# Moving the row maximum of a random-feature attention from a subtraction on k to a factor on v, with the k projection as row-tiled pairs and two load buffers for v

## The chip, the cores and the metric

The kernel runs on one core of one Trainium2 chip. The metric is the device time of one execution in microseconds (us), told as the median of several runs. The profile is one execution, recorded by the hardware profiler. PE is TensorE (PEld its weight loads), DVE is VectorE, ACT is ScalarE, POOL is GpSimd, SP is SyncE (here only an issuer of DMAs).

## The reference, cut to what matters

Eight batches of eight heads, 576 rows of 64 numbers each, go through random-feature attention (128 features), then through a gated feed-forward layer of 512 to 1536 to 512.

```
def phi(x):                       # x already scaled
    proj = einsum('bhsd,md->bhsm', x, omega)
    h = proj - sum(x * x, -1) / 2
    return exp(h - max(h, -1)) / sqrt(m)
q_p, k_p = phi(q), phi(k)
kv  = einsum('bhsm,bhsd->bhmd', k_p, v);   z = sum(k_p, axis=2)
num = einsum('bhsm,bhmd->bhsd', q_p, kv);  den = einsum('bhsm,bhm->bhs', q_p, z)
x   = num / den                   # then (gelu(x Wg) * (x Wv)) Wo
```

The term `sum(x*x)/2` is the same for all features of a row, so it falls out of `h - max(h)`. For q the whole maximum cancels in `num / den`. For k it does not: each row s carries a factor exp(-max of row s), which has to be either in the features or, as in the change, on the rows of v and on the column of ones that gives z.

## The kernel before: the parts that matter

The ones column is the 65th column of each head of `v_ext`, so one matmul gives both kv and z. PSUM is split: `att` has two buffers for all attention results, `mo` has four for the feed-forward layer.

```
ld   = tile_pool("ld", bufs=2);  work = tile_pool("work", bufs=2)
att  = tile_pool("att", bufs=2, space=PSUM);  mo = tile_pool("mo", bufs=4, space=PSUM)

def load_kq(b):  # k then q of a batch, f32 in HBM to bf16, issued by GpSimd on its queue
    ...
def load_v(b):   # f32, issued by SyncE on its own queue, ONE buffer; cast by GpSimd
    vf  = ld.tile([P, H, R * D], F32, name="vf", bufs=1)
    vrf = ld.tile([P, 4, D], F32, name="vrf", bufs=1)
    nc.sync.dma_start(out=vf, in_=v[b, ...])
    ...
    nc.gpsimd.tensor_copy(ve[:, :, :, :D], vf...)      # v_ext, its ones column set once
    ...

kq = {0: load_kq(0)};  vx = {0: load_v(0)}
...
kq[1] = load_kq(1);  vx[1] = load_v(1)

def k_feat(ps, dst, n):
    nmax = work.tile([P, n, 1], F32, name="nmax", bufs=4)
    nc.vector.reduce_max(nmax, ps, axis=AX, negate=True)
    kd = work.tile([P, n, M], F32, name="kd", bufs=5)
    nc.vector.tensor_add(kd, ps, nmax.broadcast_to((P, n, M)))
    nc.scalar.activation(dst, kd, func=Exp)

for hp in range(H // 2):                               # four groups of k rows
    pk = att_tile([P, 8, M], F32, "pk")
    for i in range(4):                                 # omega2T: omega twice, block diagonal
        nc.tensor.matmul(pk[:, 2*i:2*i+2, :], kT[:, 4*hp+i, :], omega2T)
    k_feat(pk, k_p[...], 8)
pkr = ...                                              # the last 64 rows of each head, the same
if not on_dma:                                         # batches 0 and 1 only
    qT = transpose_main(q_in, "q")                     # TensorE transposes into an att buffer
for hp in range(H // 2):                               # q features: a row-tiled pair each
    for r2 in range(2):
        sl = slice(r2 * D, (r2 + 1) * D)
        nc.tensor.matmul(pq[:, r2, :], omegaT2[sl], qT[sl, 4*hp:4*hp+4, :])
    nc.scalar.activation(q_pT[...], pq, func=Exp)
...                                                    # kz = k_p^T [v, 1], then nd = q_p kz
attention(0)
for t in range(9):                                     # the steady part
    load of batch t+2; attention(t+1); project_out(t-1); gate_val(t)
```

The softmax here doesn't subtract the row's maximum and nothing guards it: scores larger than these inputs give would overflow.

## Time and profile before

| | before |
|---|---|
| median time | 399.5 us (3 runs, 398.19 to 399.78; the prediction starts from it) |
| PE busy | 355.4 us, 89% of the span |
| DVE busy | 224.2 us, 56% |
| k rows on DVE: reduce / subtract | 32 x 1216 ns / 32 x 1215 ns |
| first projection of k (first `pk`) | 17.34 us |
| first `kz` matmul of batch 0 / of batch 1 | 35.48 / 68.09 us |
| one steady pass (from a batch's first `pk` to the next's) | 38.19 us |

The page of the kernel before: the busy line of its part 1; two of the slice lines (each digit is a fortieth of the span, in tenths: PE's busy share and the granted clock of TensorE); the chain of waits; three groups (line, engine, operation, output<-input, shape, count, then busy us and mean ns of one, then the idle time before and who ended it).

```profile
PE 355.4 (89%) x2212; PEld 174.2 (44%) x2249; DVE 224.2 (56%) x345; ACT 154.6 (39%) x202; POOL 63.0 (16%) x87
...
PE   0446756999999999999999999999999999999995
...
PEclk9999985899999999999999999999999999999999
...
PE 80%; DVE 9%; DMA 4%; issue 2%; ACT 2%; POOL 1%; SPq 0%; DVEq 0%; POOLq 0%
...
L219 DVE TENSOR_REDUCE nmax<-pk 128x8 f32<-128x1024 f32 x32 | 37.6, 1216 | 1.1 <-PE pk L227 1.1
L221 DVE TENSOR_TENSOR kd<-pk,nmax 128x1024 f32<-128x1024 f32 x32 | 37.5, 1215 | 0.0
...
L227 PE MATMUL pk<-omega2T,kT 128*128 128x256 bf16 x128 | 20.0, 294 | 5.0 <-DVE kd L221 4.9
```

From the eighth slice on PE is at 9 tenths: there the kernel is mostly bound by matmuls, and an engine such as DVE has time to spare on average. Only the first seven slices, about 70 us, are a chain of dependences, and the timeline shows what it is made of. The lines below are start, length, engine, line, what, count, and in brackets how long the engine had been idle and what ended that.

```profile
17.18 0.37 PE L206 MATMUL rT_ps<-ident,q_in 128*128 128x128 bf16 x2 [3.79 <-DMA q_in<-in_q_dram]
17.34 1.91 PE L227 MATMUL pk<-omega2T,kT 128*128 128x256 bf16 x8
...
18.44 2.36 DVE L219 TENSOR_REDUCE nmax<-pk 128x8 f32<-128x1024 f32 x2 [0.43 <-PE pk L227]
20.71 2.35 DVE L221 TENSOR_TENSOR kd<-pk,nmax 128x1024 f32<-128x1024 f32 x2
...
21.99 2.17 PE L227 MATMUL pk<-omega2T,kT 128*128 128x256 bf16 x8 [2.73 <-DVE kd L221]
...
27.82 1.87 PE L187 MATMUL qT_ps<-ident,q_in 128*128 128x128 bf16 x16 [0.61 <-DVE kd L221]
```

PE waits for the last of q (17.18), fills both attention buffers (17.34), and then stands until DVE has reduced and subtracted (21.99). Everything after follows DVE, up to the transposes of q at 27.82, which need one of the same two buffers.

### The profile page before, as it was taken

Reading aid. Unit: us, or ns where it says so; the run is one execution under the profiler, and the core shown is the slowest. Engines: PE = TensorE matmul, PEld = TensorE weight load, DVE = VectorE, ACT = ScalarE, POOL = GpSimd, SP = SyncE. Lnnn points to the kernel's source line nnn. Section 1 sums busy time; section 2 is a strip of 40 time slices with the busy share of each in tenths; the row PEclk is TensorE's granted clock in tenths of the full one; section 3 lists DMA queues with packets and bytes.
Section 4 is the critical chain, followed back from the end, with each engine's and each line's share of the span. In section 5 each row is a group of like instructions: output and inputs, shape, how many; then the busy total and the mean of one; then the engine's idle time right before and its main releaser. Section 6 shows DMA issues by size and latency. Waiting matters only on the chain.

```text
span 398.3 us, 5658 instructions
## 1 busy us (share of the span) xinstructions
PE 355.4 (89%) x2212; PEld 174.2 (44%) x2249; DVE 224.2 (56%) x345; ACT 154.6 (39%) x202; POOL 63.0 (16%) x87
## 2 busy tenths in 40 slices
PE   0446756999999999999999999999999999999995
PEld 0323523545444544444444444454535444444442
DVE  1392593748574956495559546864776423433332
ACT  1044027234833482447335633653464312311310
POOL 7563422600222041104100200000000000000000
PEclk9999985899999999999999999999999999999999
DMA  9999999980799089909992820371022012002004
GB/s 179 234 213 219 206 232 154 192 157 0 142 158 209 8 144 225 150 11 189 167 150 47 185 49 1 70 176 35 0 88 58 16 33 72 2 27 81 0 10 95
DMA packets 89626, 43.65 MB, mean 110 GB/s; under 512 B 55808, under 2 KB 84992, under 8 KB 89600
## 3 DMA queue, kind: packets, MB, share of 16 engines
q1 hardware_dynamic: 59504, 29.14, 34.2%
q0 software_dynamic: 30096, 14.16, 28.1%
q8 instruction: 17, 0.28, 0.3%
q14 instruction: 9, 0.07, 0.1%
HBM read 37.78 MB, written 9.44 MB: 119 GB/s over the span
## 4 chain that ended last, share of the span: by engine, by line
PE 80%; DVE 9%; DMA 4%; issue 2%; ACT 2%; POOL 1%; SPq 0%; DVEq 0%; POOLq 0%
PE g_ps L327 23%; PE v_ps L333 23%; PE o_ps L357 21%; DVE nmax L219 3%; DMA q_in<-in_q_dram 3%; DVE kd L221 3%; PE pk L227 3%; PE nd L276 2%; PE kz_ps L261 2%; PE pq L243 2%; ACT q_pT L245 2%; DMA out_dram<-o_sb 1%; PE qT_ps L187 1%; DVE x_sb L281 1%; DVE o_sb L360 1%
## 5 line engine op out<-in xcount | busy, mean ns | idle before, releaser
L335 DVE TENSOR_TENSOR gated<-g_gelu,v_ps 128x512 bf16<-128x512 bf16 x108 | 73.8, 683 | 86.2 <-PE v_ps L333 80.9
L330 ACT ACTIVATE g_gelu<-g_ps 128x512 bf16<-128x512 f32 x108 | 64.4, 597 | 141.2 <-PE g_ps L327 133.1
L327 PE MATMUL g_ps<-xT,w_gate_sb 128*128 128x512 bf16 x419 | 116.0, 382 | 1.5 <-issue 0.4
L333 PE MATMUL v_ps<-xT,w_val_sb 128*128 128x512 bf16 x417 | 109.9, 379 | 1.2 <-issue 0.6
L357 PE MATMUL o_ps<-w_out_sb,gated 128*128 128x512 bf16 x423 | 98.6, 379 | 0.4
L222 ACT ACTIVATE k_p<-kd 128x1024 bf16<-128x1024 f32 x32 | 33.8, 1057 | 77.6 <-DVE kd L221 76.4
L333 PEld LDWEIGHTS <-w_val_sb 128*128 128x128 bf16 x432 | 41.3, 98 | 46.9 <-issue 0.5
L357 PEld LDWEIGHTS <-gated 128*128 128x128 bf16 x432 | 41.3, 98 | 45.7 <-issue 2.7
L327 PEld LDWEIGHTS <-w_gate_sb 128*128 128x128 bf16 x432 | 40.3, 98 | 44.6 <-issue 3.7
L360 DVE COPY o_sb<-o_ps 128x512 f32<-128x512 f32 x36 | 24.2, 686 | 40.8 <-PE o_ps L357 21.2
L219 DVE TENSOR_REDUCE nmax<-pk 128x8 f32<-128x1024 f32 x32 | 37.6, 1216 | 1.1 <-PE pk L227 1.1
L221 DVE TENSOR_TENSOR kd<-pk,nmax 128x1024 f32<-128x1024 f32 x32 | 37.5, 1215 | 0.0
L245 ACT ACTIVATE q_pT<-pq 128x1024 bf16<-128x1024 f32 x32 | 30.0, 1023 | 3.9 <-PE pq L243 3.9
L227 PE MATMUL pk<-omega2T,kT 128*128 128x256 bf16 x128 | 20.0, 294 | 5.0 <-DVE kd L221 4.9
L281 DVE TENSOR_TENSOR x_sb<-nd,iden 128x512 bf16<-128x512 f32 x32 | 21.5, 688 | 0.4
L72 POOL DMA_DIRECT2D k_in<-in_k_dram x8 | 7.3, 914 | 80.1 <-DMA kT<-k_in 79.1
L227 PEld LDWEIGHTS <-kT 128*128 128x128 bf16 x128 | 11.8, 103 | 14.4 <-DVE kd L221 11.4
L243 PE MATMUL pq<-qT,omegaT_109 64*128 64x512 bf16 x64 | 13.9, 440 | 4.6 <-DVE qT L190 2.6
L265 DVE CAST kz<-kz_ps 128x520 bf16<-128x520 f32 x8 | 5.6, 698 | 20.0 <-PE kz_ps L261 20.0
L276 PEld LDWEIGHTS <-q_pT 128*128 128x128 bf16 x256 | 11.3, 104 | 9.2 <-DVE x_sb L281 3.8
L276 PE MATMUL nd<-kz,q_pT 128*128 128x65 bf16 x256 | 13.4, 203 | 1.6 <-DVE kz L265 1.2
L72 POOL DMA_DIRECT2D q_in<-in_q_dram x8 | 7.2, 906 | 36.0 <-DMA qT<-q_in 16.4
(69 smaller groups left out, 192.1 us busy)
## 6 DMA issues: line engine op xcount, KB each, us to landing
vf<-in_v_dram SPq DMA_DIRECT2D x8, 1024.0 KB, 8.7
out_dram<-o_sb SPq DMA_DIRECT2D x40, 128.0 KB, 2.4
k_in<-in_k_dram POOLq DMA_DIRECT2D x8, 512.0 KB, 9.1
q_in<-in_q_dram POOLq DMA_DIRECT2D x8, 512.0 KB, 10.6
out_dram<-o_sb SPq DMA_DIRECT2D x16, 256.0 KB, 2.9
w_gate_sb<-in_moe_w_gate_dram POOLq DMA_DIRECT2D x3, 512.0 KB, 15.0
w_val_sb<-in_moe_w_val_dram POOLq DMA_DIRECT2D x3, 512.0 KB, 14.3
w_out_sb<-in_moe_w_out_dram POOLq DMA_DIRECT2D x3, 512.0 KB, 18.9
```

The lines of the kernel that those rows point to most:

```text
L219: nc.vector.reduce_max(nmax, ps, axis=AX, negate=True)
L221: nc.vector.tensor_add(kd, ps, nmax.broadcast_to((P, n, M)))
L222: nc.scalar.activation(dst, kd, func=Exp)
L227: nc.tensor.matmul(pk[:, 2 * i:2 * i + 2, :], kT[:, 4 * hp + i, :], omega2T)
L245: nc.scalar.activation(q_pT[:, hp].rearrange("m a c p -> m a (c p)"), pq, func=Exp)
L276: nc.tensor.matmul(nd[:, h // 4, (h % 4) * DP1:(h % 4 + 1) * DP1], q_pT[:, h // 2, r2, 2 * (h % 2) + rp, :], kz_h(h))
L327: nc.tensor.matmul(g_ps, w_gate_sb[:, jm, fs], xT[:, jm, :], start=(jm == 0), stop=(jm == N_DM - 1))
L330: nc.scalar.activation(g_gelu, g_ps, func=Gelu)
L333: nc.tensor.matmul(v_ps, w_val_sb[:, jm, fs], xT[:, jm, :], start=(jm == 0), stop=(jm == N_DM - 1))
L335: nc.vector.tensor_mul(gated[:, jf, :], g_gelu, v_ps)
L357: nc.tensor.matmul(o_ps, gated[:, jf, qq * P:(qq + 1) * P], w_out_sb[:, jf, :], start=(jf == 0), stop=(jf == N_DFF - 1))
L360: nc.vector.tensor_copy(o_sb, o_ps)
```

## The change

The intent is to take the subtraction (half of what DVE does for k) away. Exp reads the projection straight from PSUM; the maximum is still reduced by DVE, but goes through a small Exp into weights `wk`, with which DVE multiplies v; GpSimd copies them into the ones column (for the last 64 rows DVE does that too). GpSimd's casts of v go. The k projection becomes pairs of 64-row matmuls that can run side by side, as q's was already. Since the cast of v now needs the maximum, v stays in its f32 buffer for longer, and the change gives v two buffers. The diff, cut to its core:

```
     def load_v(b):
-        vf = ld.tile([P, H, R * D], F32, name="vf", bufs=1)
-        vrf = ld.tile([P, 4, D], F32, name="vrf", bufs=1)
+        vf = ld.tile([P, H, R * D], F32, name="vf")          # the pool's two buffers
+        vrf = ld.tile([P, 4, D], F32, name="vrf")
...
-        nc.gpsimd.tensor_copy(ve[:, :, :, :D], vf...)        # and two for vrf
...
-        def k_feat(ps, dst, n): reduce_max, tensor_add, Exp
         for hp in range(H // 2):
-                nc.tensor.matmul(pk[:, 2*i:2*i+2, :], kT[:, 4*hp+i, :], omega2T)
+                for r2 in range(2):
+                    sl = slice(r2 * D, (r2 + 1) * D)
+                    nc.tensor.matmul(pk[:, r2, i, :], kT[sl, 4*hp+i, :], omegaT2[sl])
+            nc.scalar.activation(k_p[:, hp]..., pk..., func=Exp)
+            nc.vector.reduce_max(nmax[:, :, 4*hp:4*hp+4], pk, axis=AX, negate=True)
+            if hp == 2:
+                nc.scalar.activation(wk[:, :, :8], nmax[:, :, :8], func=Exp)
...                                                           # pkr the same
             nc.scalar.activation(q_pT[...], pq, func=Exp)
+            if hp == 0:
+                nc.scalar.activation(wk[:, :, 8:], nmax[:, :, 8:], func=Exp)
...
+        for hh in range(2):
+            isl = slice(8 * hh, 8 * hh + 8)
+            nc.vector.tensor_mul(vei[:, isl, :, :D], vfi[:, isl], wki[:, isl]...broadcast)
+            nc.gpsimd.tensor_copy(vei[:, isl, :, D], wki[:, isl])
...                                                           # v_rbd the same, on DVE
```

More of the change, by code (lines that the diff above doesn't have):

```diff
@@ L89 @@
         nc.vector.memset(v_rbd[i], 0.0)
-        nc.vector.memset(v_ext[i][:, :, :, D:DP1], 1.0)
-        for e in range(2):
-            nc.vector.memset(v_rbd[i][e * SR:(e + 1) * SR, :, e, D:DP1], 1.0)
     def load_v(b):
-        vf = ld.tile([P, H, R * D], F32, name="vf", bufs=1)
-        vrf = ld.tile([P, 4, D], F32, name="vrf", bufs=1)
+        vf = ld.tile([P, H, R * D], F32, name="vf")
+        vrf = ld.tile([P, 4, D], F32, name="vrf")
         nc.sync.dma_start(
@@ L103, in load_v @@
                     .rearrange("j s d -> s j d"))
-        ve, vr = v_ext[b % 2], v_rbd[b % 2]
-        nc.gpsimd.tensor_copy(ve[:, :, :, :D],
-                              vf.rearrange("p h (r d) -> p h r d", r=R))
-        for e in range(2):
-            sl = slice(e * SR, (e + 1) * SR)
-            nc.gpsimd.tensor_copy(vr[sl, :, e, :D], vrf[sl])
-        return ve, vr
+        return vf, vrf
     omega_f = singles.tile([M, D], F32)
@@ L123 @@
     omegaT2 = singles.tile([2 * D, M], BF16)
-    omega2T = singles.tile([2 * D, 2 * M], BF16)
-    nc.vector.memset(omega2T, 0.0)
     for e in range(2):
@@ L128 @@
         nc.vector.tensor_copy(omegaT2[sl], omegaT_ps)
-        nc.vector.tensor_copy(omega2T[sl, e * M:(e + 1) * M], omegaT_ps)
     w_gate_sb = singles.tile([P, N_DM, d_ff], BF16)
@@ L194, in attention @@
         k_both, k_in, k_rest, q_both, q_in, q_rest = kq.pop(b)
-        ve, vr = vx.pop(b)
+        vf, vrf = vx.pop(b)
+        ve, vr = v_ext[b % 2], v_rbd[b % 2]
         on_dma = b > 1
@@ L211, in attention @@
             krT, qrT = rT[:, :2], rT[:, 2:]
-        k_p = work.tile([P, H, R, M], BF16, name="k_p")
-        k_pr = work.tile([P, 4, M], BF16, name="k_pr")
-        def k_feat(ps, dst, n):
-            nmax = work.tile([P, n, 1], F32, name="nmax", bufs=4)
-            nc.vector.reduce_max(nmax, ps, axis=AX, negate=True)
-            kd = work.tile([P, n, M], F32, name="kd", bufs=5)
-            nc.vector.tensor_add(kd, ps, nmax.broadcast_to((P, n, M)))
-            nc.scalar.activation(dst, kd, func=Exp)
+        k_p = work.tile([P, H // 2, 2, 4, M], BF16, name="k_p")
+        k_pr = work.tile([P, 2, 2, M], BF16, name="k_pr")
+        nmax = work.tile([P, 2, 18], F32, name="nmax")
+        wk = work.tile([P, 2, 18], F32, name="wk")
         for hp in range(H // 2):
-            pk = att_tile([P, 8, M], F32, "pk")
+            pk = att_tile([P, 2, 4, M], F32, "pk")
             for i in range(4):
-                nc.tensor.matmul(pk[:, 2 * i:2 * i + 2, :], kT[:, 4 * hp + i, :], omega2T)
-            k_feat(pk, k_p[:, 2 * hp:2 * hp + 2].rearrange("p h r m -> p (h r) m"), 8)
-        pkr = att_tile([P, 4, M], F32, "pkr")
-        for jj in range(2):
-            nc.tensor.matmul(pkr[:, 2 * jj:2 * jj + 2, :], krT[:, jj, :], omega2T)
-        k_feat(pkr, k_pr, 4)
+                for r2 in range(2):
+                    sl = slice(r2 * D, (r2 + 1) * D)
+                    nc.tensor.matmul(pk[:, r2, i, :], kT[sl, 4 * hp + i, :], omegaT2[sl])
+            nc.scalar.activation(k_p[:, hp].rearrange("p a i m -> p a (i m)"),
+                                 pk.rearrange("p a i m -> p a (i m)"), func=Exp)
+            nc.vector.reduce_max(nmax[:, :, 4 * hp:4 * hp + 4], pk, axis=AX, negate=True)
+            if hp == 2:
+                nc.scalar.activation(wk[:, :, :8], nmax[:, :, :8], func=Exp)
+        pkr = att_tile([P, 2, 4, M], F32, "pkr")
+        for jj in range(2):
+            for j2 in range(2):
+                sl = slice(j2 * D, (j2 + 1) * D)
+                nc.tensor.matmul(pkr[:, j2, jj, :], krT[sl, jj, :], omegaT2[sl])
+        nc.scalar.activation(k_pr, pkr[:, :, :2], func=Exp)
+        nc.vector.reduce_max(nmax[:, :, 16:], pkr[:, :, :2], axis=AX, negate=True)
         if not on_dma:
@@ L251, in attention @@
         nc.scalar.activation(q_pTr.rearrange("m a c p -> m a (c p)"), pqr[:, :, :256], func=Exp)
+        vei = ve.rearrange("p h (c r) d -> p (h c) r d", r=2)
+        vfi = vf.rearrange("p h (c r d) -> p (h c) r d", c=2, r=2)
+        wki = wk.rearrange("p r i -> p i r")
+        for hh in range(2):
+            isl = slice(8 * hh, 8 * hh + 8)
+            nc.vector.tensor_mul(vei[:, isl, :, :D], vfi[:, isl],
+                                 wki[:, isl].unsqueeze(3).broadcast_to((P, 8, 2, D)))
+            nc.gpsimd.tensor_copy(vei[:, isl, :, D], wki[:, isl])
+        for e in range(2):
+            sl = slice(e * SR, (e + 1) * SR)
+            vre = vr[sl, :, e, :].rearrange("p (a j) d -> p a j d", j=2)
+            nc.vector.tensor_mul(vre[..., :D],
+                                 vrf[sl].rearrange("p (a j) d -> p a j d", j=2),
+                                 wki[sl, 16:].unsqueeze(3).broadcast_to((SR, 2, 2, D)))
+            nc.vector.tensor_copy(vre[..., D], wki[sl, 16:])
         kz_ps = att_tile([P, 2, 512], F32, "kz_ps")
@@ L256, in attention @@
             g, c0 = j // 2, (j % 2) * 2 * DP1
-            nc.tensor.matmul(kz_ps[:, g, c0:c0 + 2 * DP1], k_pr[:, j, :],
+            nc.tensor.matmul(kz_ps[:, g, c0:c0 + 2 * DP1], k_pr[:, j % 2, j // 2, :],
                              vr[:, j].rearrange("p e c -> p (e c)"), start=True, stop=False)
@@ L261, in attention @@
                     nc.tensor.matmul(kz_ps[:, g, c0 + e * DP1:c0 + (e + 1) * DP1],
-                                     k_p[:, 2 * j + e, r, :], ve[:, 2 * j + e, r, :],
+                                     k_p[:, j, r % 2, 2 * e + r // 2, :], ve[:, 2 * j + e, r, :],
                                      start=False, stop=(e == 1 and r == R - 1))
```

## The prediction

> **What bounds the kernel now.** TensorE (PE): 89% busy on the page, the chain of waits is 67% the three feed-forward lines, and from 74 us on every slice shows 9 tenths. In the timeline one pass (attention of a later batch, project_out, gate_val) takes 38.19 us (o_ps runs begin at 92.74, 130.93, 169.12): 144 feed-forward matmuls at 216 ns are 31.1, attention the other 7.1. Only the head, to 72 us, is a dependency chain: for k of batch 0 VectorE (DVE) runs without gap from 18.44 to 29.0 us (reduce 1216 ns, add 1215 ns, four groups); batch 1 repeats it from 51.14 to 61.7.
>
> **Removed.** The subtraction: 32 x 1215 + 8 x 683 ns = 43 us of DVE; the v casts on GpSimd (21.6 us).
>
> **Added.** Per batch two 1024-element f32 multiplies on DVE (estimate 1.2 us each, as the kd add) and small ones (1 us): DVE falls by some 15 us. Two tiny Exps (estimate 0.25 us each). In the k projection 18 matmuls of 256 columns (108 ns apart in the steady part) become 18 row pairs of 128.
>
> **PE, steady part.** pq is such a pair already: its matmuls begin 3 ns apart, so a k pair should cost 55 to 66 ns (a load plus 65 columns of kz go every 33 ns). Gain 18 x 48 = 0.8 us per batch. But o_ps to pq takes 312 ns in place of 216, and pq to o_ps 320 after a 213 ns stream: 0.2 us per row-tiled run. The Trainium skill, "TensorEngine Tiling (Array Packing)", Key Properties, says that changing mode drains the array; the trace agrees. In the built order the k projection lies in four separate runs per batch: 0.8 us of new switches. Net: I take -0.3 us over six batches.
>
> **Head.** A pk buffer was held for two DVE operations (2.43 us). Now Exp (1.02) and reduce (1.22) read it, and the built order makes the reduce wait for ScalarE. With two buffers, and the first v multiply ahead of the fourth reduce, my schedule frees the last pk buffer 1.7 to 2.0 us earlier per batch, not 5; the extra Exp takes back 0.25. So kz comes 1.5 to 1.8 us earlier after the first pk in batches 0 and 1.
> But v of batch 1 no longer waits for a buffer: its load falls into 10 to 17 us beside k and q of batch 0, and PE starts pk only when the last of q has landed (17.15 us). Estimated slip, by packet rates: 1.2 to 1.7 us. Batch 0 then gains almost nothing.
>
> **Sum.** 399.5 - 0.2 (batch 0) - 1.6 (batch 1) - 0.3 (steady) = about 397.3 us; 8 in 10 between 394.0 and 400.4. Chances: faster by over 2% 0.05, within 0.92, slower 0.03.
>
> **What would show it.** First pk at 18.5 to 19 us, not 17.34. Idle before nmax ended by ScalarE. DVE near 210 us. kz of batch 0 at 35 to 35.6 us (35.48 before), of batch 1 near 66.5 (68.09). A pass of 38.0 to 38.4 us. Switches of 0.1 us at pk.
>
> **What would make it wrong.** Pairs not overlapping (110 ns each: +5 us). q landing unmoved (1.5 us more gain). The half-rate PE clock of 56 to 73 us ending elsewhere (1 to 2 us). A reduce or o_sb copy late in the steady part, stalling PE at pkr or pq, where the schedule leaves about 0.5 us.

## The result, and the profile after

The changed kernel takes 395.34 us (median of 4 runs, 394.74 to 395.64) against 399.25 us (398.19 to 399.78, 4 runs) of the kernel before in the same rounds. The ratio is 0.9903, with a 95% interval of 0.9879 to 0.9928. A ratio here is the mean time of one kernel's fast runs over that of the other's of the same rounds, so not quite the ratio of the medians. The result is correct.

The page of the changed kernel, in the same lines as above:

```profile
PE 353.2 (90%) x2393; PEld 167.8 (43%) x2393; DVE 213.3 (54%) x344; ACT 154.5 (39%) x218; POOL 47.9 (12%) x79
...
PEclk9999975999999999999999999999999999999999
...
PE 86%; DVE 5%; DMA 3%; ACT 3%; issue 1%; POOL 1%; POOLq 0%
...
L214 ACT ACTIVATE k_p<-pk 128x1024 bf16<-128x1024 f32 x32 | 31.9, 1023 | 41.9 <-PE pk L213 41.8
L216 DVE TENSOR_REDUCE nmax<-pk 128x8 f32<-128x1024 f32 x32 | 37.9, 1220 | 13.0 <-ACT k_p L214 13.0
...
L213 PE MATMUL pk<-omegaT_100,kT 64*128 64x128 bf16 x256 | 12.3, 228 | 3.6 <-DVE nmax L216 3.6
```

DVE's share of the chain falls from 9% to 5%, and the wait before the reduce is now for ScalarE (13.0 us) where it was 1.1 us for PE: Exp and reduce read a buffer one after the other. The timeline of the head shows the same, and two things more.

```profile
18.60 0.37 PE L196 MATMUL rT_ps<-ident,q_in 128*128 128x128 bf16 x2 [4.19 <-DMA q_in<-in_q_dram]
18.91 1.19 PE L213 MATMUL pk<-omegaT_100,kT 64*128 64x128 bf16 x16
...
19.56 1.94 ACT L214 ACTIVATE k_p<-pk 128x1024 bf16<-128x1024 f32 x2 [17.53 <-PE pk L213]
20.61 2.35 DVE L216 TENSOR_REDUCE nmax<-pk 128x8 f32<-128x1024 f32 x2 [1.18 <-ACT k_p L214]
21.89 0.61 PE L213 MATMUL pk<-omegaT_100,kT 64*128 64x128 bf16 x8 [1.79 <-DVE nmax L216]
...
24.73 1.22 DVE L254 TENSOR_TENSOR v_ext_70<-vf,wk 128x1024 bf16<-128x1024 f32 x1
...
25.87 1.22 DVE L216 TENSOR_REDUCE nmax<-pk 128x8 f32<-128x1024 f32 x1
...
27.14 1.87 PE L176 MATMUL qT_ps<-ident,q_in 128*128 128x128 bf16 x16 [1.87 <-DVE nmax L216]
```

First, the last of q lands 1.4 us later (18.60 against 17.18). Second, DVE does a multiply of v (24.73) before the last group's reduce (25.87), while PE stands waiting for that reduce to free a buffer. Where the 5.16 us between the two profiled spans (398.34 and 393.18 us) come from, read off the starts in the two timelines:

| stretch | before, us | after, us | difference |
|---|---|---|---|
| start to first pk | 17.34 | 18.91 | +1.57 |
| first pk to kz, batch 0 | 18.14 | 16.03 | -2.11 |
| kz of batch 0 to pk of batch 1 | 15.03 | 14.89 | -0.14 |
| pk to kz, batch 1 | 17.58 | 15.56 | -2.02 |
| kz of batch 1 to pk of batch 2 | 23.61 | 22.88 | -0.73 |
| pk of batch 2 to the end | 306.64 | 304.91 | -1.73 |

Five steady passes take 37.96 us each in place of 38.19 or 38.20 (the last of the five 38.44), which makes most of the last line. The profiled run of before was a long one (400.12 us, against its median of 399.25), so the traces are further apart than the medians.

### The profile page after: what moved, and what is told of

The parts are those of the page before. It is cut to its first block, busy times and chain, and to the rows that moved or that the text cites. A ratio compares the mean times of both kernels' runs of the same rounds, so it can differ in the third digit from the quotient of the medians.

```text
span 393.2 us, 5990 instructions
## 1 busy us (share of the span) xinstructions
PE 353.2 (90%) x2393; PEld 167.8 (43%) x2393; DVE 213.3 (54%) x344; ACT 154.5 (39%) x218; POOL 47.9 (12%) x79
## 4 chain that ended last, share of the span: by engine, by line
PE 86%; DVE 5%; DMA 3%; ACT 3%; issue 1%; POOL 1%; POOLq 0%
PE o_ps L369 25%; PE g_ps L339 24%; PE v_ps L345 24%; DMA q_in<-in_q_dram 3%; PE kz_ps L273 2%; PE pk L213 2%; PE nd L288 2%; PE pq L236 2%; ACT k_p L214 2%; ACT q_pT L238 1%; DVE nmax L216 1%; PE qT_ps L176 1%; DVE x_sb L293 1%; PE kz_ps L269 1%; DVE qT L179 1%
## 5 line engine op out<-in xcount | busy, mean ns | idle before, releaser
L339 PE MATMUL g_ps<-xT,w_gate_sb 128*128 128x512 bf16 x432 | 113.5, 381 | 0.4 <-DVE xT L151 0.4
L345 PE MATMUL v_ps<-xT,w_val_sb 128*128 128x512 bf16 x432 | 113.0, 379 | 0.0
L369 PE MATMUL o_ps<-w_out_sb,gated 128*128 128x512 bf16 x432 | 106.0, 380 | 0.0
L339 PEld LDWEIGHTS <-w_gate_sb 128*128 128x128 bf16 x432 | 41.7, 98 | 47.2 <-issue 0.7
L369 PEld LDWEIGHTS <-gated 128*128 128x128 bf16 x432 | 37.5, 98 | 44.1 <-issue 5.4
L214 ACT ACTIVATE k_p<-pk 128x1024 bf16<-128x1024 f32 x32 | 31.9, 1023 | 41.9 <-PE pk L213 41.8
L216 DVE TENSOR_REDUCE nmax<-pk 128x8 f32<-128x1024 f32 x32 | 37.9, 1220 | 13.0 <-ACT k_p L214 13.0
L213 PE MATMUL pk<-omegaT_100,kT 64*128 64x128 bf16 x256 | 12.3, 228 | 3.6 <-DVE nmax L216 3.6
L213 PEld LDWEIGHTS <-kT 64*128 64x128 bf16 x256 | 8.0, 98 | 12.9 <-issue 12.3
L273 PEld LDWEIGHTS <-k_p 128*128 128x128 bf16 x256 | 12.1, 107 | 0.4 <-issue 0.4
L256 POOL CAST v_ext_71<-wk 128x16 bf16<-128x16 f32 x8 | 3.1, 390 | 72.3 <-ACT wk L218 60.8
```

The source lines that it names most:

```text
L213: nc.tensor.matmul(pk[:, r2, i, :], kT[sl, 4 * hp + i, :], omegaT2[sl])
L214: nc.scalar.activation(k_p[:, hp].rearrange("p a i m -> p a (i m)"), pk.rearrange("p a i m -> p a (i m)"), func=Exp)
L216: nc.vector.reduce_max(nmax[:, :, 4 * hp:4 * hp + 4], pk, axis=AX, negate=True)
L339: nc.tensor.matmul(g_ps, w_gate_sb[:, jm, fs], xT[:, jm, :], start=(jm == 0), stop=(jm == N_DM - 1))
L345: nc.tensor.matmul(v_ps, w_val_sb[:, jm, fs], xT[:, jm, :], start=(jm == 0), stop=(jm == N_DM - 1))
L369: nc.tensor.matmul(o_ps, gated[:, jf, qq * P:(qq + 1) * P], w_out_sb[:, jf, :], start=(jf == 0), stop=(jf == N_DFF - 1))
```

## The experiments

All twelve kernels gave correct results. "First pk", "kz" and "pk of batch 2" are start times in each trace, in us. The same changed kernel gave 0.9903 and 0.9916, and each ratio has an interval of about 0.002 to 0.003 to either side; so a difference of two ratios is good to about 1 us, and the start times in the traces carry the finer comparisons.

| kernel | time | before beside it | ratio, 95% interval | first pk | kz, batch 0 | pk, batch 2 | pass |
|---|---|---|---|---|---|---|---|
| before | 399.25 | | | 17.34 | 35.48 | 91.70 | 38.19 |
| changed | 395.34 | 399.25 | 0.9903 (0.9879, 0.9928) | 18.91 | 34.94 | 88.27 | 37.96 |
| e1 no pairs | 398.65 | 400.04 | 0.9958 (0.9939, 0.9978) | 18.87 | 35.75 | 90.30 | 38.22 |
| e2 pairs only | 399.63 | 400.04 | 0.9999 (0.9982, 1.0015) | 16.98 | 34.57 | 90.19 | 38.41 |
| e3 one v buffer | 391.49 | 400.04 | 0.9791 (0.9765, 0.9818) | 14.55 | 30.58 | 83.16 | 37.96 |
| e4 late weight Exp | 394.24 | 400.04 | 0.9852 (0.9829, 0.9875) | 19.07 | 33.91 | 87.46 | 37.96 |
| e5 before, two v buffers | 405.08 | 399.52 | 1.0147 (1.0127, 1.0167) | 21.68 | 39.81 | 96.97 | 38.19 |
| e6 = e3 + e4 | 388.72 | 399.52 | 0.9734 (0.9709, 0.9759) | 14.38 | 29.22 | 82.22 | 37.96 |
| e7 = e6, v behind q | 388.72 | 399.52 | 0.9728 (0.9706, 0.9750) | 12.33 | 27.18 | 81.58 | 37.96 |
| e8 reads split by bank | 400.83 | 399.52 | 1.0039 (1.0020, 1.0058) | 19.08 | 36.53 | 93.04 | 38.20 |
| e9 = e6, maximum from SBUF | 387.45 | 399.40 | 0.9687 (0.9655, 0.9719) | 14.84 | 27.39 | 79.77 | 38.06 to 39.53 |
| e10 = all of it | 384.48 | 399.40 | 0.9620 (0.9586, 0.9653) | 12.30 | 24.86 | 75.85 | 38.21 to 38.41 |
| e11 = e10, SBUF form in the head only | 381.98 | 399.99 | 0.9558 (0.9539, 0.9577) | 12.15 | 24.71 | 74.91 | 37.96 |
| e12 changed, again | 396.31 | 399.99 | 0.9916 (0.9899, 0.9933) | 19.41 | 35.44 | 89.81 | 37.96 |

### Are the pairs worth anything? (e1, e2)

My theory: the pairs save 18 x 48 ns or a little more per batch on PE and lose most of that at four changes of tiling. The rival: the shorter pass comes from DVE being free. e1 takes the pairs out of the changed kernel; e2 puts the pairs alone into the kernel before.

```
e1, against the changed kernel              e2, against the kernel before
-  for r2 in range(2):                      -  matmul(pk[:, 2*i:2*i+2, :], kT[...], omega2T)
-      matmul(pk[:, r2, i, :],              +  for r2 in range(2):
-             kT[sl, ...], omegaT2[sl])     +      matmul(pk[:, r2, i, :],
+  matmul(pk[:, i], kT[...], omega2T)       +             kT[sl, ...], omegaT2[sl])
   (layouts of k_p, nmax and wk follow)        (reduce, subtraction and Exp as before)
```

> The changed kernel with the k projection undone: full-width matmuls of 256 columns against the block-diagonal omega, everything else kept. Theory (the pairs shorten a steady pass by about 0.2 us: 18 x 54 ns gained, four switches of 0.19 us lost): pass back at 38.15 to 38.25 us, time 1.2 to 2.0 us above the changed kernel's (396.5 to 397.4). Rival A (the shorter pass came from the new order of PE and the missing subtraction, the pairs are worth nothing): pass stays at 37.96, time within 0.5 us of the changed kernel.

> The kernel before with nothing but the row-tiled pairs; the subtraction, the v casts and their buffers stay. Theory: pass falls from 38.19 to about 37.96 us, the head stays DVE-bound (kz of batch 0 at 35.2 to 35.5, of batch 1 near 67.8), time 1.2 to 2.0 us below before. Rival A: pass stays at 38.2, time within 0.5 us of before.

In e1 the pass behaved as the theory has it: it went from 37.96 to 38.22 us. The time was longer than foretold (398.65 us, not 396.5 to 397.4). By the ratios (0.9958 and 0.9903) e1 is 2.2 us slower than the changed kernel. The traces show about 6 x 0.26 us of passes, and, not in my sum, 0.85 and 0.40 us in the heads of the two first batches (pk to kz 16.88 and 15.96 us in place of 16.03 and 15.56): together 2.8 us, within the uncertainty of the ratios.

In e2 the time was the rival's (0.4 us below before by the medians, a ratio of 0.9999), but the pass was neither's: it became longer, 38.41 us. The head hid that: pk of batch 2 comes 1.5 us earlier than before (90.19 against 91.70), and the six longer passes give most of it back. The pairs are worth 0.26 us per pass in the changed kernel and minus 0.22 us in the kernel before. The view of waits of PE's weight loads, taken over the five steady passes (columns: total us, times, longest), shows why. In the kernel before:

```profile
PEld L227 <- DVE kd L221: 3.9, 10, 0.4
```

with the pairs alone:

```profile
PEld L226 <- DVE kd L218: 5.5, 10, 0.6
...
PEld L232 <- DVE kd L218: 2.9, 5, 0.6
```

and in the changed kernel:

```profile
PEld L213 <- issue: 6.4, 15, 0.4
```

With the subtraction in place a buffer comes free only when DVE has made both passes over it. A quicker PE only arrives earlier at that wait: it now waits longer before pk and also before pkr. In the trace of one pass of e2 the starts from an `o_ps` matmul to the next `pk` or `pkr` are 299, 144 and 244 ns beyond the normal distance, where the drain alone is 95; that is 0.40 us in excess, and the pass is 0.45 us longer than 37.96. In the changed kernel no load of k is released by DVE in the steady part at all. So the pairs and the removal of the subtraction belong together; each alone gives no shorter pass than before (38.41 and 38.22 against 38.19), both give 37.96.

The drain itself: the Trainium skill, "TensorEngine Tiling (Array Packing)", Key Properties, says that changing the tiling mode drains TensorE. The trace agrees: an `o_ps` matmul of 216 ns is followed by the next one after 216 ns, but by the first pair of a `pk` run after 312. Going in costs 95 ns and coming out about 94. The pair itself takes 54 ns instead of 108. Two runs of one pass, before and after:

```profile
129.89 1.04 PE L227 MATMUL pk<-omega2T,kT 128*128 128x256 bf16 x8
130.76 3.62 PE L357 MATMUL o_ps<-w_out_sb,gated 128*128 128x512 bf16 x16
```

```profile
126.23 0.62 PE L213 MATMUL pk<-omegaT_100,kT 64*128 64x128 bf16 x16
126.78 3.41 PE L369 MATMUL o_ps<-w_out_sb,gated 128*128 128x512 bf16 x15
```

From the first pk to the next o_ps it is 0.87 us before and 0.55 after. Per batch: 18 x 54 ns = 0.97 us won, four runs x 0.19 us = 0.76 us lost, 0.21 us net; the passes differ by 0.23.

### What does the second v buffer cost? (e3, e5)

The theory from the prediction: with two buffers, v of batch 1 is loaded while k and q of batch 0 are still on their way, and takes bandwidth from q. e3 gives the changed kernel its one buffer back; e5 gives the kernel before two buffers and changes nothing else.

```
e3, against the changed kernel        e5, against the kernel before
-  vf = ld.tile(..., name="vf")       -  vf = ld.tile(..., name="vf", bufs=1)
+  vf = ld.tile(..., bufs=1)          +  vf = ld.tile(..., name="vf")
   (vrf likewise)                        (vrf likewise)
```

> The changed kernel with one load buffer for v, as before, so v of batch 1 is loaded only after the v multiplies of batch 0. Theory (the early load of v for batch 1 delays the landing of q of batch 0 by 1.4 us, and that is the start of the chain): the last q lands near 17.2, first pk at 17.3 to 17.6 in place of 18.91, all later marks of the head 1.2 to 1.5 us earlier, time 1.0 to 1.5 us below the changed kernel. Rival B (the slip is absorbed later, or v of batch 1 now comes late): first pk early, but kz of batch 1 where it was or later, time same or longer.

> The kernel before with nothing but two load buffers for v. Theory (the second buffer lets v of batch 1 share the DMA engines with k and q of batch 0): the first pk slips from 17.34 to 18.5 to 19.2 us, the head marks after it slip with it, time 0.8 to 1.8 us above before. Rival B (the slip in the changed kernel has another cause, for example that GpSimd no longer casts v and issues its loads sooner): first pk stays at 17.0 to 17.6, time as before.

Both moved in the foretold direction, and by far more than I had foretold: e3 is 4.5 us faster than the changed kernel (0.9791 against 0.9903), and e5 is 5.9 us slower than the kernel before. The first pk comes at 14.55 and 21.68 us. The issue times of v's second load explain the size. In the kernel before, the cast on GpSimd frees the buffer early, and v of batch 1 is issued at

```profile
8.79 0.38 SPq L97 DMA_DIRECT2D vf<-in_v_dram  x1
```

in the changed kernel it needs no buffer to come free:

```profile
3.11 0.74 SPq L95 DMA_DIRECT2D vf<-in_v_dram  x1
```

and in e3 it has to wait until the multiply has read the first v, so the way is clear for q:

```profile
14.55 1.19 PE L213 MATMUL pk<-omegaT,kT 64*128 64x128 bf16 x16
...
29.02 0.40 SPq L95 DMA_DIRECT2D vf<-in_v_dram  x1
```

I had compared the changed kernel with the kernel before only, and overlooked that even the kernel before has this collision: of the load issued at 8.79 us the first packets move at 12.59 us. Up to 12 us the queue of k and q had moved as much there as in e3 (2,324 packets against 2,318), at 14 us 2,940 against 3,329. That speaks against GpSimd's missing casts as the cause of the earlier q in e3. In e5 the buffer is freed by the cast at 9 us, so a third v load is issued at 9.08 us, and q of batch 0 lands at 21.5 us.

Why one load hurts another so much shows in the DMA records, counted in stretches of 2 us by queue (k, q and weights share one queue, v has the other):

```
                      k/q queue               v queue
changed, 10 to 12 us  431 packets, 0.097 MB   436 packets, 0.446 MB
changed, 12 to 14 us  418 packets, 0.117 MB   412 packets, 0.419 MB
one buffer, 10 to 12  918 packets, 0.390 MB   none
```

The two queues send nearly as many packets each, but not as many bytes. A packet of v has 1,024 bytes, those of k and q in this stretch 4 to 512. The Trainium skill, "DMA: Bandwidth & Descriptors", Queues, rings and completion order, says that each DMA engine goes round the queues that have work at the granularity of packets; the equal counts agree with that, though the trace does not show where an engine changes over, and a packet of the page can hold several transfers. The trace adds what it means here: a load with large packets takes 0.446 of 0.543 MB in the stretch and halves the packets of the load that is being waited for.

### What does the place of the small Exp cost? (e4, e6)

In the changed kernel the first small Exp sits before the last group's Exp on ScalarE. It makes the weights early, so the built order (the order in which the build put DVE's instructions) has the first multiply of v before the last reduce, and that reduce is what frees the buffer for the transposes of q.

```
e4, against the changed kernel (e6 is e4 with one v buffer)
-            if hp == 2:
-                nc.scalar.activation(wk[:, :, :8], nmax[:, :, :8], func=Exp)
...
         nc.scalar.activation(k_pr, pkr[:, :, :2], func=Exp)
+        nc.scalar.activation(wk[:, :, :8], nmax[:, :, :8], func=Exp)
```

> The changed kernel with the first Exp of the maxima issued after the Exp of the last k rows, so that the first v multiply stands behind all reduces. Theory (that multiply, 1.22 us, sits between the third and fourth reduce and holds back the last pk buffer, on which the q transposes wait): q transposes near 26.0 and 56.5 in place of 27.14 and 57.64, kz of each head batch about 1.1 us earlier per batch, time about 2.0 us below the changed kernel; steady pass unchanged at 37.96. Rival C (the v multiplies then end last before kz): q transposes earlier but kz not, time within 0.5 us of the changed kernel.

> The changed kernel with one v buffer and the late Exp of the maxima together. If the two gains add (start of the chain 4.4 us earlier; last pk buffer free about 1.1 us earlier in each head batch): first pk near 14.5, kz of batch 0 near 29.5, of batch 1 near 58.2, time 389 to 390 us, 6 us below the changed kernel. If they share one cause or a DMA landing becomes the next limit (k of batch 1, weights), time stays at 391 to 392.

In e4 the multiply stands behind the reduces, and the transposes of q no longer wait for it:

```profile
23.75 2.36 DVE L216 TENSOR_REDUCE nmax<-pk 128x8 f32<-128x1024 f32 x2 [0.62 <-ACT k_p L214]
...
26.16 1.86 PE L176 MATMUL qT_ps<-ident,q_in 128*128 128x128 bf16 x16 [0.74 <-DVE nmax L216]
...
26.70 1.22 DVE L253 TENSOR_TENSOR v_ext<-vf,wk 128x1024 bf16<-128x1024 f32 x1
```

They begin 7.09 us after the first pk in place of 8.23, kz 14.84 in place of 16.03, and the same again in batch 1 (14.42 in place of 15.56). That is 2.0 us of time (0.9852 against 0.9903), as two heads of about 1.1 us would have it. The two edits add up: e6 has 0.9734, which is 6.8 us below the changed kernel, and 4.5 + 2.0 = 6.5. The time, 388.72 us, is just under the 389 to 390 that I had written.

### Can v wait behind q altogether? (e7)

```
-        nc.sync.dma_start(out=vf, ...)
+        eng = nc.gpsimd if b == 0 else nc.sync        # k's and q's queue for batch 0
+        eng.dma_start(out=vf, ...)
```

> As the kernel with one v buffer and late Exp, but v of batch 0 is issued on the queue of k and q, behind them. If DMA time before the last q is all that sets the first pk, that queue has the engines alone from the start: its packets end near 11.5 us in place of 13.3, first pk 12.5 to 13.2, time 1.3 to 2.0 us below that kernel. Against it: v of batch 0 then lands near 16 to 18 us, and if that is after its multiply wants it, or the queue alone does not reach the rate of two, nothing is gained.

The first pk came at 12.33 us, 2.05 us earlier than in e6, yet the time is the same (0.9728 against 0.9734). The gain met a new wait:

```profile
27.91 0.42 POOL L256 CAST v_ext<-wk 128x16 bf16<-128x16 f32 x2
...
28.25 0.60 PE L273 MATMUL kz_ps<-v_ext,k_p 128*128 128x65 bf16 x8 [0.81 <-POOL v_ext L256]
```

GpSimd fills the ones columns, and in its queue those two small casts stand behind DMA issues that themselves wait for q of batch 1. By the first pk of batch 2 only 0.64 us of the gain is left, and in the time nothing that the interval would show. This wait of 0.81 us is the larger part of the 1.4 us lost; the rest I did not follow.

### Is it the two readers of a buffer, one after the other? (e8, e9)

The theory for what still bounds the head: each buffer is read by Exp (1.02 us) and then by the reduce (1.22 us), so it is held for both. The Trainium skill, "PSUM — Partial Sum Buffer", PSUM bank collisions raise a hardware error, says that two engines must not be in one bank (of the same 32 partitions) at once, not even both reading. The built order keeps to that (the reduce waits 13.0 us for ScalarE in the group above); no run here shows a collision. e8 tried to let the two read different banks of the buffer at the same time.

```
e8, against the changed kernel
-            nc.scalar.activation(k_p[:, hp], pk, func=Exp)
-            nc.vector.reduce_max(nmax[:, :, 4*hp:4*hp+4], pk, ...)
+            for a in range(2):                    # Exp on bank a, reduce on the other
+                nc.scalar.activation(k_p[:, hp, a], pk[:, a], func=Exp)
+                nc.vector.reduce_max(nmax[:, 1-a, 4*hp:4*hp+4], pk[:, 1-a], ...)
```

> The changed kernel with Exp and reduce each split by PSUM bank, so that ScalarE reads one bank of pk while VectorE reads the other, then they change over. Theory (the two readers of pk stand one after the other, so a buffer is held for 2.25 us): the hold falls to about 1.4 us, q transposes follow the first pk by about 7.0 us in place of 8.2, in both head batches, time about 2 us below the changed kernel. Rival D (VectorE itself or the extra instructions limit: twice as many of half the size): q transposes within 0.3 us of where they were, time within 0.7 us of the changed kernel.

It missed both expectations, and tells nothing about the theory. The built order waits for the whole tile, not for a bank, so four smaller operations run one after another:

```profile
19.73 0.60 ACT L215 ACTIVATE k_p<-pk 128x512 bf16<-128x512 f32 x1 [17.71 <-PE pk L213]
20.36 0.69 DVE L217 TENSOR_REDUCE nmax<-pk 128x4 f32<-128x512 f32 x1 [0.75 <-ACT k_p L215]
21.08 1.08 ACT L215 ACTIVATE k_p<-pk 128x512 bf16<-128x512 f32 x2 [0.76 <-DVE nmax L217]
```

Each half takes more than half the time (0.60 of 1.02 us, 0.69 of 1.22 us), the buffer is held longer (the transposes of q come 9.70 us after the first pk, not 8.23), the pass is 38.20 us, and the time is 400.83 us.

e9 tests the theory another way: the maximum is read from the exponentials in SBUF. Exp is monotonic, so the maximum of the exponentials is the exponential of the maximum, and the weight is its reciprocal. PSUM then has one reader.

```
e9, against e6
-            nc.vector.reduce_max(nmax[...], pk, axis=AX, negate=True)
+            nc.vector.reduce_max(nmax[...], k_p[:, hp], axis=AX)
...
-        nc.scalar.activation(wk[:, :, :8], nmax[:, :, :8], func=Exp)    # and the other
+        nc.vector.reciprocal(wk, nmax)
```

> The one-buffer kernel with the late weight exponential, and the maximum is read from the exponentials in SBUF in place of the k rows in PSUM (the weights are then the reciprocal of that maximum, one operation on VectorE, and the two small exponentials on ScalarE go). A pk buffer is then held by one reader (Exp, about 1.0 us) and not by two in a row (1.0 + 1.2 us). Theory (two serial readers of the pk buffers pace the head of each pass): the first q transpose copy comes 4.6 to 5.2 us after the first pk (7.09 before this edit), kz about 12.4 us after it (14.84), the same again in batch 1, the steady pass stays at 37.9 to 38.1; time 383.5 to 386.0. Rival (VectorE's reduces, in order before its q copies, pace the head): kz still 14.3 to 15 us after the first pk, time 387.5 to 389.5.

The head did what the theory said: the transposes of q came 4.47 us after the first pk (7.09 before the edit), kz 12.55 after it (14.84), and 12.13 in batch 1. The weights now come from exponentials rounded to bf16, and the result stayed correct. The first line below is ScalarE, which now runs four Exps in a row; the reduces follow one Exp behind, and the transposes of q wait for ScalarE, not for DVE. The last line is from batch 2.

```profile
15.48 3.77 ACT L214 ACTIVATE k_p<-pk 128x1024 bf16<-128x1024 f32 x4 [13.47 <-PE pk L213]
16.54 4.60 DVE L216 TENSOR_REDUCE nmax<-k_p 128x8 f32<-128x1024 bf16 x4 [1.18 <-ACT k_p L214]
...
19.31 1.86 PE L176 MATMUL qT_ps<-ident,q_in 128*128 128x128 bf16 x16 [0.52 <-ACT k_p L214]
...
93.00 0.42 PE L270 MATMUL kz_ps<-v_ext,k_p 128*128 128x65 bf16 x8 [1.30 <-POOL v_ext L253]
```

The time missed: 387.45 us, at the lower edge of what I had written for the rival (387.5 to 389.5). Its seven runs spread from 386.47 to 391.47 us, wider than any other kernel's, and the traced one, 389.42 us, was a long one. pk of batch 2 is 2.45 us earlier than in e6, but the pass after it takes 39.53 us and the others 38.06 to 38.19. The last line shows 1.30 us of the long pass: GpSimd's ones columns again, this time behind its issue of the next k. The reduce is no quicker from bf16 in SBUF (1211 ns against 1220); the Trainium skill, "VectorE: DVE Perf Modes", The perf-mode tier table, gives `tensor_reduce` no faster mode for any type, and the trace agrees.

### Everything together, and the steady part left alone (e10, e11)

e10 is e7 with the maximum from SBUF and the ones columns copied by VectorE. e11 is e10 with that form in batches 0 and 1 alone.

```
e11, against e10
+            if on_dma:                              # from batch 2 on
+                nc.vector.reduce_max(nmax[...], pk, axis=AX, negate=True)
+            else:
                 nc.vector.reduce_max(nmax[...], k_p[:, hp], axis=AX)
...              (weights and ones columns likewise: e6's way if on_dma, else e10's)
```

> The same maximum from SBUF, together with v of batch 0 behind k and q on the same queue and the ones columns copied by VectorE in place of GpSimd. Theory: first pk at 12.2 to 12.5 us, no wait for GpSimd before the first v_ext matmuls, kz of batch 0 near 24.8, time 381.5 to 384.5. Rival (as in the kernel with v behind q, the 2 us won at the first pk are lost to the next wait in the head): time within 0.7 us of the kernel with one v buffer and the maximum from SBUF.

> The kernel with everything combined, but with the maximum read from SBUF (and the ones columns on VectorE) only in batches 0 and 1, the chain of dependences; from batch 2 on the maximum is read from PSUM again, as in the changed kernel with the late weight exponential. Theory (the passes of 38.2 to 38.4 us come from the SBUF form of the maximum in the steady part, not from the earlier start): passes of 37.9 to 38.0 us, head as before this edit (first pk 12.2 to 12.5, kz of batch 0 24.7 to 25.1, first pk of batch 2 near 75.8), time 382.3 to 383.8. Rival (the longer pass goes with the earlier head, whatever the form): passes of 38.2 to 38.4, time 384.0 to 385.2.

e10 gave 384.48 us, at the upper end of the theory's range; kz of batch 0 came at 24.86 us and no wait for GpSimd stood before it. The first pk is 2.54 us earlier than in e9 and pk of batch 2 is 3.92 us earlier, so this time the gain of the earlier q is kept up to there. But the passes are then 38.2 to 38.4 us, and the time is 2.7 us below e9 by the ratios (0.9620 against 0.9687), 3.0 by the medians. e11 answers why: with the head unchanged (kz at 24.71) and the steady part as in e6, the passes are 37.96 again, and the time is 381.98 us, just under the 382.3 that I had put as the lower end. So it is the form of the steady part that lengthens the pass, and not the earlier head. e11 takes two things back there at once, the maximum from SBUF and the ones columns on VectorE; that e9, with the ones columns still on GpSimd, also has passes of 38.06 us and more suggests that the maximum from SBUF has a part in it, but they were not separated. What in the order of PE's work does it, I did not follow. e11 is the best version: 4.4% below the kernel before.

### The changed kernel a second time (e12)

> A control: the changed kernel, not edited, timed a second time on this chip beside the kernel before. If the first comparison holds: 394.5 to 396.0 us and a ratio of 0.988 to 0.993; the granted clock 0.982 or 0.983 in nearly all of its runs, where the kernel before has 0.977 or 0.978 in most.

The ratio is 0.9916, inside the range; the median, 396.31 us, is 0.3 us above it. All its runs had a granted clock of 0.983, those of the kernel before 0.977 or 0.978 in nine of eleven. That clock is a real part of the times. In the traces TensorE is granted half its clock for 17.07 us in the head before (from 56.09 us on) and for 13.65 us after; in e11 it is 6.83 us. The Trainium skill, "TensorE: Matmul & The Clock Gate", Part 1: The HAM clock gate, gives a free-running window of 3413 ns after which the clock may change. The trace agrees: these are five, four and two such windows. Of 42 runs of the kernel before, 33 had a mean clock of 0.977 or 0.978 and a mean time of 399.9 us; 9 had 0.981 or 0.982, and 398.7. A mean clock higher by 0.004 is one such window (an estimate: half of 3.413 us in 398), so one window less goes with 1.2 us less, at the same code.

This is also in the -0.73 us from kz of batch 1 to pk of batch 2, but what it goes with there is the half-clock time that falls into the stretch, not the number of windows: 5.07 us before, 3.29 us after. Over the twelve traces whose steady part reads the maximum from PSUM (all but e9 and e10) the stretch is about 21.4 us and 0.44 us more for each us at half clock in it, to within 0.11 us. e4, with four windows as the changed kernel, has 5.04 us of it, and its stretch takes 23.68 us, as long as before. Whether the shorter head causes the earlier return to the full clock was not tested.

## Why the prediction was right or wrong

The class (within 2% of before) and the range were right: 395.3 and 396.3 us lie within 394.0 to 400.4. The centre, 397.3 us, was 2 us too high. Every term of the sum was too small a gain, so no two errors cancelled; that the time stayed inside is owed to a range 6.4 us wide.

- **What bounds the kernel.** Right. The steady part was bound by PE before and after, so 11 us less of DVE (224.2 to 213.3; I wrote "near 210") did not appear as 11 us.
- **"First pk at 18.5 to 19 us, not 17.34."** Right: 18.91; the second trace has 19.41, a little above it. The cause was shown by e3 and e5. What I missed is that the collision costs far more than the 1.57 us of difference, since the kernel before has part of it too: without it the first pk is at 14.55 us.
- **"Idle before nmax ended by ScalarE."** Right: 13.0 us, all of it. That it bounds the head was shown by e9.
- **"kz comes 1.5 to 1.8 us earlier after the first pk in batches 0 and 1."** The mechanism held, the size was low: 2.11 and 2.02 us. "kz of batch 0 at 35 to 35.6" was 34.94 in the trace (35.44 in the second); "batch 1 near 66.5" was 65.39 (66.61 in the second).
- **"-0.3 (steady)."** The step that failed most. I had costed a gain of 18 x 48 ns and a loss of four runs x 0.2 us, and called it nearly even. Measured are 18 x 54 ns and 4 x 0.19 us, so 0.21 us are left per pass, the passes are shorter by 0.23, and six of them make 1.4 us and not 0.3. "A pass of 38.0 to 38.4" was 37.96. Both numbers were in the right place; their difference was too small to be taken from rounded terms.
- **"Switches of 0.1 us at pk."** Right: 95 ns in, 94 out.
- **"The half-rate PE clock ... ending elsewhere (1 to 2 us)."** Named as a risk, and it came: one window less in all, and 1.78 us less of half clock in the stretch whose difference is 0.73 us.

The terms, against the traces: batch 0 -0.54 (I had -0.2), batch 1 -0.14 - 2.02 = -2.16 (-1.6), the stretch with the clock -0.73 (none), the rest -1.73 (-0.3). Together -5.16 where I had -2.1, of which 0.9 is that the profiled run of before was longer than its median.

## What to carry to other kernels

When an edit removes a wait for a buffer, ask which transfer that wait was holding back, and what it will now run beside: here the second v buffer, which looks harmless, cost 4.5 us, more than the whole edit gained. Two improvements of one loop can each leave its pass no shorter alone (pairs without the shorter buffer turn, the shorter turn without pairs), so undo them one at a time before calling one of them useless. And what helps a chain of dependences can cost in the part that is bound by throughput: e11 uses one form of the same maximum in the head and another in the steady part, and is the fastest for it.

## What the Trainium skill lacked or had wrong

- "TensorEngine Tiling (Array Packing)", Key Properties, says that a change of mode drains, but not what that costs. Here it is 95 ns in and about 94 out between 512-column matmuls, 0.19 us per run of pairs, which took 0.76 of the 0.97 us that the pairs gained per batch.
- "DMA: Bandwidth & Descriptors", Queues, rings and completion order, describes the turn by packets (431 against 436 packets in 2 us agree with it), but does not draw the conclusion: a queue with 1,024-byte packets took 0.446 MB beside 0.097 MB of the queue with smaller ones, and that queue's load was late by 4.4 us (first pk at 18.91 against 14.55).
- "TensorE: Matmul & The Clock Gate", Part 1, has the 3413 ns window right (five, four and two of them). One window more or less in the head goes with 1.2 us in 400, from run to run of the same kernel.
- No page that I read says that reading a row maximum from the exponentials in SBUF frees a PSUM buffer earlier: about 2.3 us per head of a batch here (kz 12.55 us after the first pk in place of 14.84).
